# A new order of loads in the opening: both k loads, both q, v, then raw weights on SP, p of the first batch on ScalarE's queue

## The chip, the cores and the metric

The kernel runs on one core of one Trainium2 chip. The metric is the device time of one execution in microseconds (us); several runs give a median. Beside them stands one profiled execution, from which all rows below are read.

## What is computed

Three stages follow each other. Attention of 8 batches of 8 heads, 576 rows of 64, through 32 packed rows `p`; then three products and their maximum, and an output product; then a softplus layer with its output product.

```python
scale = 1.0 / np.sqrt(q.shape[-1])
def sm_attn(qq, kk, vv):
    s = scale * np.matmul(qq, kk.transpose(0, 1, 3, 2))
    s = s - np.max(s, axis=-1, keepdims=True)
    a = np.exp(s)
    a = a / (np.sum(a, axis=-1, keepdims=True) + 1e-09)
    return np.matmul(a, vv)
p_packed = sm_attn(p, k, v)
x = sm_attn(q, p_packed, p_packed)          # then as 4608 x 512
h = np.maximum(np.maximum(x @ w1, x @ w2), x @ w3)
x = h @ w_out
h = x @ w_in
out = (np.maximum(h, 0.0) + np.log1p(np.exp(-np.abs(h)))) @ w_out2
```

## The kernel before

One program works through the batches one after the other. The work of a batch is cut into steps with short names, and a string of names sets the order in which their instructions are written; every engine takes its own instructions in that order. The string of the opening, `order`, holds batch 0 and the preparation of batch 1, beside the narrowing of the weights; the string of the later batches is not touched.

The steps that matter here: `Lk`, `Lq`, `Lv`, `Lp` load k, q, v and p of a batch (`Lk00` and `Lk02` are the two halves of k of batch 0, four heads each; `Lk10`, `Lk12` those of batch 1), `LW` loads a block of a raw weight. `PP` transposes p on TensorE (L269) and ScalarE copies it out of PSUM (L284). `Tk` and `Tq` transpose two heads of k or q (L238, nine matmuls each), and ScalarE or VectorE copies them (L248, L246; the set `on_vector` says which). `S` forms the scores of the packed rows (L311), `SX` their maximum and exponential (L331, L337), `E` transposes those (L358, L365), `V` multiplies with v (L385), `VS` scales (L401), `PT` transposes the packed rows again (L269, L277), `A` forms the scores of q against them (L311), `AX` their exponentials. `PW` multiplies the packed rows with the weights (L486), and `U` are the large products of the second stage (L510). `N` and `NT` narrow a raw weight on ScalarE (L85), GpSimd (L95) and VectorE (L111).

All loads of before are issued by SP, one behind the other. A load waits for one of eight completion semaphores, `DMAHW0` to `DMAHW7`, which are used in turn: a load waits until the load eight places ahead of it has landed. Pools add waits of their own: five buffers for k and q (`rx`), five for raw weights (`stp`), four PSUM tiles (`mm`).

The table `lead` says how many idle transposes of the identity (L166) TensorE does ahead of a step; their results are not read.

Of the kernel before, what the change touches and what calls it, by code (L numbers as in the profile page):

```python
# [19 lines left out]
def packed_attention_maxout_softplus(  # L20
# [22 lines left out]
    nc = tc.nc  # L43
# [113 lines left out]
    ps1, psv, ps2, on_gpsimd, on_vector, lead = {}, {}, {}, set(), set(), {}  # L157
# [51 lines left out]
    def load_p(n):  # L209
        t = tp.tile([P, NG, D], F32, tag="praw", name="praw")  # L210
        for G in range(NG):
            nc.sync.dma_start(
                out=t[:, G],
                in_=bass.AP(p.tensor, p[n, G].offset, [[NG * NP * D, NH], [D, NP], [1, D]]),
            )
        praw[n] = t
# [416 lines left out]
    def opening(name):  # L633
# [20 lines left out]
        if a == "L":  # L654
            return layer2_steps(0, i[1])
        return {
            "Lv": lambda n: once(load_v, n),
            "Lp": lambda n: once(load_p, n),
            "PP": prep_steps,
            "S": lambda n: once(scores1, n),  # L660
# [12 lines left out]

    on_gpsimd.update(
        """
        AX00.sb AX00.mu X00 AX01.sb AX01.mu X01 AX10.sb AX10.mu X10 SO2 SO5 LS02
        LS03 LS04
        """.split()
    )
    on_vector.update("Tk03 Tq00 Tq01 Tq02 Tq03 Tk12".split())  # L680
    lead.update({'Tk00': 12, 'Tk02': 3, 'V0': 14, 'PT0': 3, 'A0': 2, 'Tk10': 14, 'S1': 6, 'U1': 2})
    order = """
            Lk00 Lp0 Lp1 Lk02 LW10 Lq00 Lq02 Tk00 Lv0 LW02 LW00 LW01 PP0 Tk00 Tk01 PP0 Lk10 Tk02
            Tk01 Tk03 Tk02 Lk12 NT10 N10 PP1 Tk03 PP1 S0 N10 LW12 Tq01 SX00 SX01 SX00 LW20 Tq00
            SX01 Tq00 E00 Tq02 VS00 E00 Tq01 E01 Tq02 Tq03 VS01 E01 Tq03 V0 NT02 N02 VS01 VS00
            PT0 N02 PT0 LW11 N00 A0 NT00 PT0 N00 LW21 AX00 NT01 N01 AX00 AX01 AX00 Tk10 AX01
            AX00 N01 AX01 Tk11 Tk10 LW22 AX00 Tk13 AX01 AX00 Tk11 AX00 AX01 Tk12 Tk13 AX01 PW00
            AX01 AX00 N12 Tk12 X00 NT20 S1 AX01 PW00 X00 X01 PW00 N20 U1 X01 SX10 N11 U0 N20
            SX10 NT11 U0 LW30 SX11 N21 NT21 E10 N11 U0 NT12 U1 E10 LW32 N21 NT22 U2 N22 LW31 N12
            U2 SX11 LW50 N22 PW01 LW41 VS11 NT30 N30 U1 E11 PW01 U2 U3 NT32 PW01 N32 U3 E11 U7  # L690
            VS10 N31 N32 NT31 LW40 N31 U3 U6 LS00 LW42 N30 NT50 N50 LW51 LS00 PW02 U6 N50 NT41
            N41 U5 LO3 U7 PW02 N41 LW52 U4 PW02 N40 NT40 N40 U11 LO1 U4 NT42 N42 U5 U8 N42 LS01
            NT51 LO0 N51 LS01 PW03 N51 SO3 ST3 LO2 U8 U9 PW03 Lv1 SO3 SO3 NT52 LO4 PW03 U10 N52
            N52 U9 ST1 U12 LS02 LO5 SO3 Lq11 SO1 LS02 U10 PW04 SO1 U12 U14 ST0 PW04 Lq10 U11 ST2
            SO1 PW04 LS03 U13 SO1 SO2 LS03 SO0 SO2 U15 SO0 SO2 U13 SO2 SO0 U16 U14 U15 SO0 V1
            LS04 U16 ST4 SO4 LS04 U17 VS11 VS10 SO5 SO4 Lq13 ST5 PT1 SO4 U17 LS05 SO5 SO4 SO5
            Lq12 PT1 LS05 SO5 L21 Tq10 Lp2 Tq11 PW10 L21 Lk20 Tq13 L22 PW10 PW10 Lk21 Tq12 D0
            Lk23 A1 L22 D1 L20 AX10 AX10 AX11 AX10 AX11 AX10 AX11 AX10 AX11 AX10 L23 L20 AX11 AX10
            D2 AX11 Lk22 AX10 AX11 X10 X10 AX11 X11 X11 L23
    """  # L700
    E = mybir.EngineType
    under_way = {}
# [128 lines left out]
    def in_batch(n, name):  # L831
# [8 lines left out]
        if a == "Lp":  # L840
            return once(load_p, m + 1) if m + 1 < B else none
# [516 lines left out]
```

## Time and profile before

| | before |
|---|---|
| median of 3 runs | 1206.23 us (1204.69 to 1206.42) |
| profiled execution | 1205.73 us, span 1203.9 us |
| TensorE busy in the span | 1186.9 us, 99% |
| VectorE, ScalarE, GpSimd busy | 837.1, 528.6, 228.2 us |

TensorE is busy almost throughout, and of its 17 us without work most lie ahead of 45 us. The time of the profiled execution is 1.8 us longer than its span, and 0.5 us below the median. Times in the rows count from the start of the span. The granted clock is given as a share of 2.4 GHz: 1.00 is that level, 0.50 is 1.2 GHz.

### The profile page before, as it was taken

To read this page: it belongs to the slowest core of one execution; us is meant where nothing else is said; L and a number is where in the kernel's file an instruction comes from. 1 tells how busy PE (TensorE), PEld (TensorE's weight loads), DVE (VectorE), ACT (ScalarE), POOL (GpSimd) and SP (SyncE) were. 2 spreads that over 40 slices of the span, in tenths; PEclk is the share of its full clock that TensorE was granted. 3 is DMA by queue.
4 is the path that set the end of the run, shared out by engine and by line. 5 is a ranking of instruction groups with operands and counts; after the bars stand their busy time and mean duration, and the time that the engine had idled before them with its cause. 6 is when DMAs were issued, how large, how long until landed. Compare 5 with 4: busy or idle time off the path is not lost.

```text
span 1203.9 us, 21042 instructions
## 1 busy us (share of the span) xinstructions
PE 1186.9 (99%) x8458; PEld 1051.1 (87%) x8458; DVE 837.1 (70%) x1199; ACT 528.6 (44%) x789; POOL 228.2 (19%) x229
## 2 busy tenths in 40 slices
PE   8999999999999999999999999999999999999998
PEld 6788989898989898988888888888888899999998
DVE  3867777677776757777797457974479745874585
ACT  3744453535353624544463234543345333543343
POOL 1732332333233301151000220001200012001100
PEclk8999999999999999999999999999999999999999
DMA  9799879889898721666676955569565697778775
GB/s 274 260 219 221 238 224 238 233 222 248 219 249 218 211 92 34 243 236 258 209 247 187 330 184 184 197 188 336 198 198 173 194 368 250 241 250 325 250 251 148
DMA packets 146818, 272.24 MB, mean 226 GB/s; under 512 B 15136, under 2 KB 88352, under 8 KB 141600
## 3 DMA queue, kind: packets, MB, share of 16 engines
q1 hardware_dynamic: 144512, 269.13, 72.0%
q10 hardware_dynamic: 2208, 1.77, 0.5%
q8 instruction: 66, 1.08, 0.4%
q14 instruction: 32, 0.26, 0.1%
HBM read 218.43 MB, written 52.43 MB: 225 GB/s over the span
## 4 chain that ended last, share of the span: by engine, by line
PE 88%; DVE 5%; DMA 4%; SPq 1%; ACT 1%; issue 1%; POOL 0%; DVEq 0%; ACTq 0%; POOLq 0%
PE ps L510 29%; PE ps L1092 28%; PE ps L1187 25%; PE ps_w L486 3%; DMA woraw<-in_moe_w_out_dram 1%; DMA vt<-in_v_dram 1%; DVE glo L127 1%; PE ps_s L311 1%; DVE x2lo L127 1%; PE ps_v L385 1%; DMA wc<-wic 1%; SPq L187 1%; PE ps_e L358 1%; DVE a L1150 0%; DMA kraw<-in_k_dram 0%
## 5 line engine op out<-in xcount | busy, mean ns | idle before, releaser
L1092 PE MATMUL ps<-x2hi,wc 128*128 128x512 f32 (+1 forms) x1120 | 322.2, 367 | 0.6 <-DMA wc<-wic 0.4
L1187 PE MATMUL ps<-ghi,wc 128*128 128x512 f32 (+1 forms) x1120 | 321.6, 367 | 0.0
L1107 DVE TENSOR_TENSOR h<-h,ps 128x512 f32<-128x512 f32 (+1 forms) x280 | 171.4, 632 | 159.8 <-PE ps L1092 94.1
L1092 PEld LDWEIGHTS ps<-x2hi,wc 128*128 128x128 f32 x1120 | 207.2, 188 | 27.6 <-ACT h L1109 0.7
L1187 PEld LDWEIGHTS ps<-ghi,wc 128*128 128x128 f32 x1120 | 207.1, 188 | 26.0
L1187 PE MATMUL ps<-glo,wc 128*128 128x512 f32 (+1 forms) x560 | 206.6, 369 | 0.7 <-DVE glo L127 0.6
L1092 PE MATMUL ps<-x2lo,wc 128*128 128x512 f32 (+1 forms) x560 | 205.6, 367 | 0.0
L1128 ACT ACTIVATE a<-h 128x512 f32<-128x512 f32 (+1 forms) x160 | 89.0, 585 | 221.6 <-DVE h L1107 194.3
L125 ACT ACTIVATE ghi<-a 128x1024 fp32r<-128x1024 f32 (+1 forms) x120 | 115.8, 974 | 108.5 <-PE ps L1187 99.4
L127 DVE TENSOR_TENSOR glo<-a,ghi 128x1024 fp32r<-128x1024 f32 (+1 forms) x120 | 131.8, 1110 | 33.3 <-ACT ghi L125 33.1
L1150 POOL TENSOR_TENSOR a<-a,a 128x512 f32<-128x512 f32 (+1 forms) x32 | 36.9, 1153 | 537.7 <-ACT a L1128 537.7
L510 PE MATMUL ps<-a2hi,pwhi 128*128 128x288 f32 x576 | 128.4, 304 | 0.4 <-DVE m L540 0.3
L510 PE MATMUL ps<-a2lo,pwhi 128*128 128x288 f32 x576 | 123.2, 295 | 0.9 <-POOL a2lo L127 0.9
L510 PE MATMUL ps<-a2hi,pwlo 128*128 128x288 f32 x576 | 123.3, 295 | 0.0
L1187 PEld LDWEIGHTS ps<-glo,wc 128*128 128x128 f32 x560 | 105.1, 188 | 16.9 <-DVE glo L127 3.6
L1092 PEld LDWEIGHTS ps<-x2lo,wc 128*128 128x128 f32 x560 | 105.1, 188 | 13.2
L510 PEld LDWEIGHTS ps<-a2hi,pwhi 128*128 128x128 f32 x576 | 91.5, 189 | 16.3 <-ACT m L538 6.2
L540 DVE TENSOR_TENSOR m<-ps,m 128x576 f32<-128x576 f32 x96 | 72.4, 754 | 47.2 <-PE ps L510 44.0
L127 POOL TENSOR_TENSOR hlo<-m,hhi 128x576 fp32r<-128x576 f32 x44 | 66.0, 1501 | 199.8 <-ACT hhi L125 181.1
L510 PEld LDWEIGHTS ps<-a2lo,pwhi 128*128 128x128 f32 x576 | 92.4, 188 | 1.4 <-POOL a2lo L127 1.4
L510 PEld LDWEIGHTS ps<-a2hi,pwlo 128*128 128x128 f32 x576 | 92.5, 188 | 0.0
L510 PE MATMUL ps<-hhi,wo_hi 128*128 128x288 f32 x384 | 83.2, 298 | 0.2 <-ACT wo_hi L125 0.2
(121 smaller groups left out, 1485.9 us busy)
## 6 DMA issues: line engine op xcount, KB each, us to landing
wc<-woc SPq DMA_DIRECT2D x40, 1792.0 KB
wc<-wic SPq DMA_DIRECT2D x32, 1792.0 KB
qraw<-in_q_dram SPq DMA_DIRECT2D x112, 140.0 KB
wic<-wc SPq DMA_DIRECT2D x8, 1792.0 KB
kraw<-in_k_dram SPq DMA_DIRECT2D x96, 140.0 KB
wraw<-in_moe_w_dram SPq DMA_DIRECT2D x18, 512.0 KB
xu<-x2d SPq DMA_DIRECT2D x72, 128.0 KB
raw<-in_moe_w_out_dram SPq DMA_DIRECT2D x16, 512.0 KB
```

Of the source, the lines that this page charges most:

```text
L125: nc.scalar.activation(out=hi, in_=src, func=AF.Copy)
L127: engine.tensor_tensor(out=lo, in0=src, in1=hi.bitcast(F32), op=ALU.subtract)
L187: queue.dma_start(out=t[row : row + 32].rearrange("p t b d -> p (t b d)")[:, :size], in_=bass.AP(src.tensor, src[n, NG * g + G].offset + 3 ...
L311: nc.tensor.matmul(ps[G][cols, h, :HS], w[2][rows, G, cols] if 2 in w else w[1][rows, cols], x[rows, g, hh * HS : hh * HS + HS], start=Tru ...
L486: nc.tensor.matmul(ps[cols, G, : units * P].rearrange("p (w x) -> p w x", w=units), ppT[n][1][rows, cols], wsb[rows, 4 * c : 4 * c + units ...
L510: nc.tensor.matmul(o, w, xx, start=first, stop=last)
L540: nc.vector.tensor_tensor(out=m, in0=ps[:, :, :HS], in1=ms[n, f], op=ALU.max)
L1092: nc.tensor.matmul(out, l, r, start=(i == 0), stop=(i == len(terms) - 1))
L1107: add(out=h[:, o], in0=h[:, a], in1=ps, op=ALU.add)
L1128: nc.scalar.activation(out=g[half, k][:, j, :wide], in_=h[:, 2 * k + half], func=AF.Softplus)
L1150: engine.tensor_tensor(out=out, in0=in0, in1=in1, op=op)
L1187: nc.tensor.matmul(ps[b][:, :wide], l, r, start=first and u == 0 and head, stop=u == FP - 1 and tail, skip_group_check=not first,)
```

## The change

The two DMAs of p of batch 0 are issued by ScalarE instead of SP. The string `order` is another, from its first word to the last; the sets `on_gpsimd` and `on_vector` and the table `lead` change with it (56 idle transposes before, 54 now). The steps themselves are the same, and from the first `U` of batch 1 on TensorE's instructions stand in the same order as before.

```diff
     def load_p(n):
         t = tp.tile([P, NG, D], F32, tag="praw", name="praw")
         for G in range(NG):
-            nc.sync.dma_start(
+            (nc.scalar if n == 0 else nc.sync).dma_start(
...
-    on_vector.update("Tk03 Tq00 Tq01 Tq02 Tq03 Tk12".split())
-    lead.update({'Tk00': 12, 'Tk02': 3, 'V0': 14, 'PT0': 3, 'A0': 2, 'Tk10': 14, 'S1': 6, 'U1': 2})
+    on_vector.update("Tk01 Tk03 Tq02 Tq03 Tk12".split())
+    lead.update(
+        {'PP0': 9, 'Tk01': 2, 'Tk02': 6, 'V0': 8, 'PT0': 3, 'A0': 3, 'Tk10': 4, 'PP1': 7, 'PW00': 2, 'E11': 10}
+    )
     order = """
-            Lk00 Lp0 Lp1 Lk02 LW10 Lq00 Lq02 Tk00 Lv0 LW02 LW00 LW01 PP0 Tk00 Tk01 PP0 Lk10 Tk02
...
+            Lp0 Lk00 Lk02 Lq00 Lq02 Lv0 PP0 LW01 PP0 LW02 Tk01 Tk00 LW10 Tk02 Tk00 Tk01 Lk10
...
```

SP's queue from its first load on, before:

```order
L177 DMA kraw_123<-in_k_dram 128x1152
L212 DMA praw_125<-in_p_dram 128x1x64 x2
L212 DMA praw_128<-in_p_dram 128x1x64 x2
L177 DMA kraw_131<-in_k_dram 128x1152
L608 DMA wraw_133<-in_moe_w1_dram 128x4x256
L177 DMA qraw_135<-in_q_dram 128x1152
L177 DMA qraw_137<-in_q_dram 128x1152 [waits DMAHW0_49]
L204 DMA vt_161<-in_v_dram 32x8x384 [waits DMAHW1_49]
L204 DMA vt_161<-in_v_dram 32x8x384 [waits DMAHW2_49]
L204 DMA vt_161<-in_v_dram 32x8x384 [waits DMAHW3_49]
L608 DMA wraw_165<-in_moe_w3_dram 128x4x256 [waits DMAHW4_49]
L608 DMA wraw_167<-in_moe_w1_dram 128x4x256 [waits DMAHW5_49]
```

SP's queue from its first load on, now:

```order
L177 DMA kraw_126<-in_k_dram 128x1152
L177 DMA kraw_128<-in_k_dram 128x1152
L177 DMA qraw_130<-in_q_dram 128x1152
L177 DMA qraw_132<-in_q_dram 128x1152
L204 DMA vt_134<-in_v_dram 32x8x384 x2
L204 DMA vt_134<-in_v_dram 32x8x384 [waits DMAHW0_49]
L608 DMA wraw_152<-in_moe_w2_dram 128x4x256 [waits DMAHW1_49]
L608 DMA wraw_156<-in_moe_w3_dram 128x4x256 [waits DMAHW2_49]
L608 DMA wraw_180<-in_moe_w1_dram 128x4x256 [waits DMAHW3_49]
L177 DMA kraw_201<-in_k_dram 128x1152 [waits DMAHW4_49]
L177 DMA kraw_225<-in_k_dram 128x1152 [waits DMAHW5_49,PE_49]
L608 DMA wraw_255<-in_moe_w1_dram 128x4x256 [waits DMAHW6_49]
```

The two loads of p of batch 0 have left the queue, those of batch 1 have moved to places 13 and 14, and the first raw weight stands behind v instead of ahead of q. Of three raw weights and a load of k behind v, two (`DMAHW1`, `DMAHW3`) wait for the two halves of p of batch 0, which ScalarE issues.

ScalarE's queue from its first instruction on, before:

```order
L70 ACT_TABLE_LOAD
L248 ACTIVATE vT_176<-ps_k_139 128x576 [waits PE_49]
L284 ACTIVATE pT2_188<-ps_t_171 128x256 [waits PE_49]
L248 ACTIVATE vT_176<-ps_k_178 128x576 [waits PE_49]
L248 ACTIVATE vT_176<-ps_k_192 128x576 [waits PE_49]
```

ScalarE's queue from its first instruction on, now:

```order
L70 ACT_TABLE_LOAD
L212 DMA praw_123<-in_p_dram 128x1x64 x2
L284 ACTIVATE pT2_154<-ps_t_138 128x256 [waits PE_49]
L248 ACTIVATE vT_198<-ps_k_170 128x576 [waits PE_49]
L248 ACTIVATE vT_198<-ps_k_182 128x576 [waits PE_49]
```

The two loads of p stand behind the load of the activation tables and wait for nothing.

TensorE's order from its first instruction on, before (`kraw_123` and `kraw_131` are the halves of k, `praw_125` and `praw_128` are p of batch 0 and of batch 1):

```order
L166 MATMUL ps_k_139<-ident_65 128x128 [waits Pool_49]
L166 MATMUL ps_k_139<-ident_65 128x128 x11
L238 MATMUL ps_k_139<-ident_65,kraw_123 128x64 [waits DMAHW0_49]
L238 MATMUL ps_k_139<-ident_65,kraw_123 128x64 x8
L269 MATMUL ps_t_171<-ident_65,praw_125 64x128 [waits DMAHW1_49]
L269 MATMUL ps_t_171<-ident_65,praw_125 64x128
L269 MATMUL ps_t_171<-ident_65,praw_125 64x128 [waits DMAHW2_49]
L269 MATMUL ps_t_171<-ident_65,praw_125 64x128
L238 MATMUL ps_k_178<-ident_65,kraw_123 128x64 x9
L166 MATMUL ps_k_192<-ident_65 128x128 x3
L238 MATMUL ps_k_192<-ident_65,kraw_131 128x64 [waits DMAHW5_49]
```

TensorE's order from its first instruction on, now (`praw_123` is p of batch 0, `kraw_126` and `kraw_128` are the halves of k):

```order
L166 MATMUL ps_t_138<-ident_65 128x128 [waits Pool_49]
L166 MATMUL ps_t_138<-ident_65 128x128 x8
L269 MATMUL ps_t_138<-ident_65,praw_123 64x128 [waits DMAHW1_49]
L269 MATMUL ps_t_138<-ident_65,praw_123 64x128
L269 MATMUL ps_t_138<-ident_65,praw_123 64x128 [waits DMAHW3_49]
L269 MATMUL ps_t_138<-ident_65,praw_123 64x128
L166 MATMUL ps_k_158<-ident_65 128x128 x2
L238 MATMUL ps_k_158<-ident_65,kraw_126 128x64 [waits DMAHW0_49]
L238 MATMUL ps_k_158<-ident_65,kraw_126 128x64 x8
L238 MATMUL ps_k_170<-ident_65,kraw_126 128x64 x9
L166 MATMUL ps_k_182<-ident_65 128x128 x6
L238 MATMUL ps_k_182<-ident_65,kraw_128 128x64 [waits DMAHW2_49]
```

Ahead of the first transposes of k TensorE now waits for both halves of p (`DMAHW1`, `DMAHW3`). The transposes of p of batch 1, which stood ahead of the first scores, stand behind `A0` and the transposes of k of batch 1 now.

## Rows read from the trace of the kernel before

**Rows 1.** Windows of TensorE: window, length and busy (x), granted clock, DMA share, GB/s.

```profile
8.07:14.90 6.83, 5.85 (x70) 0.50 1.06 275
...
22.00:45.00 23.00, 19.71 (x313) 1.00 0.77 254
45.00:98.00 53.00, 51.63 (x517) 1.00 0.90 246
```

**Rows 2.** Timeline of TensorE: start us, us, line, operation, count [idle before <-releaser].

```profile
1.36 2.82 PE L166 MATMUL ps_k<-ident 128*128 128x128 f32 x12 [1.36 <-POOL ident masks.py:199]
4.21 0.94 PE L238 MATMUL ps_k<-ident,kraw 64*128 64x64 f32 x9
...
9.05 1.81 PE L238 MATMUL ps_k<-ident,kraw 64*128 64x64 f32 x18 [2.10 <-DMA kraw<-in_k_dram]
10.80 1.12 PE L269 MATMUL ps_t<-ident,praw 128*64 128x128 f32 x8
11.85 2.17 PE L311 MATMUL ps_s<-vT,pT 64*32 64x288 f32 x32
...
16.61 0.74 PE L238 MATMUL ps_k<-ident,qraw 64*128 64x64 f32 x9 [0.38 <-DMA qraw<-in_q_dram]
...
18.78 1.75 PE L166 MATMUL ps_v<-ident 128*128 128x128 f32 x14
21.93 1.55 PE L385 MATMUL ps_v<-vt,e1T 96*32 96x64 f32 x96 [1.40 <-DMA vt<-in_v_dram]
...
25.46 1.21 PE L311 MATMUL ps_s<-vT,ppT 64*32 64x288 f32 x32 [0.26 <-ACT ppT L284]
```

**Rows 3.** Timeline of the SP queue: start us, us, line, issues.

```profile
0.74 0.41 SPq L177 DMA_DIRECT2D kraw<-in_k_dram  x1
1.21 2.45 SPq L212 DMA_DIRECT2D praw<-in_p_dram  x4
3.70 0.60 SPq L177 DMA_DIRECT2D kraw<-in_k_dram  x1
...
5.83 1.85 SPq L204 DMA_DIRECT2D vt<-in_v_dram  x3
```

**Rows 4.** Timeline of ScalarE, opening.

```profile
0.73 1.28 ACT L70 ACT_TABLE_LOAD   x1 [0.73 <-PEq L1336]
...
18.18 0.81 ACT L365 ACTIVATE e1T<-ps_e 96x768 f32<-96x768 f32 x1 [1.10 <-PE ps_e L358]
```

**Rows 5.** DMA in 2.5:3.5, 4.6:5.0 and 11:14.8: packets (tenths busy ahead in 4.6:5.0).

```profile
DMA packets 87, 0.38 MB, mean 378 GB/s; under 512 B 5, under 2 KB 5, under 8 KB 87
...
DMA  3143143144134135224404413440441399253143
...
DMA packets 119, 0.05 MB, mean 117 GB/s; under 512 B 115, under 2 KB 115, under 8 KB 119
...
DMA packets 390, 0.69 MB, mean 183 GB/s; under 512 B 28, under 2 KB 345, under 8 KB 390
```

**Rows 6.** Issues of ScalarE and of SP after 496 us.

```profile
500.11 0.33 ACTq L588 DMA_DIRECT2D x2d<-xs  x1
...
504.91 0.33 ACTq L588 DMA_DIRECT2D x2d<-xs  x1
...
497.36 1.85 SPq L943 DMA_DIRECT2D wu<-wi  x1
...
500.98 1.16 SPq L943 DMA_DIRECT2D wu<-wi  x1
```

**Rows 7.** DMA by queue in 504.5:506.5, then 509.2:511.5: q1 SP, q10 ScalarE.

```profile
q1 hardware_dynamic: 74, 0.68, 79.8%
q10 hardware_dynamic: 136, 0.28, 36.1%
...
q1 hardware_dynamic: 146, 0.60, 63.5%
q10 hardware_dynamic: 133, 0.27, 30.2%
```

More of the change, by code (lines that the diff above doesn't have):

```diff
@@ L675, in packed_attention_maxout_softplus @@
         """
-        AX00.sb AX00.mu X00 AX01.sb AX01.mu X01 AX10.sb AX10.mu X10 SO2 SO5 LS02
-        LS03 LS04
+        AX00.sb AX00.mu X00 AX01.sb AX01.mu AX10.sb AX10.mu SO2 SO3 LS00 LS01 LS02
+        LS04
         """.split()
     )
-    on_vector.update("Tk03 Tq00 Tq01 Tq02 Tq03 Tk12".split())
-    lead.update({'Tk00': 12, 'Tk02': 3, 'V0': 14, 'PT0': 3, 'A0': 2, 'Tk10': 14, 'S1': 6, 'U1': 2})
+    on_vector.update("Tk01 Tk03 Tq02 Tq03 Tk12".split())
+    lead.update(
+        {'PP0': 9, 'Tk01': 2, 'Tk02': 6, 'V0': 8, 'PT0': 3, 'A0': 3, 'Tk10': 4, 'PP1': 7, 'PW00': 2, 'E11': 10}
+    )
@@ L682, in packed_attention_maxout_softplus @@
     order = """
-            Lk00 Lp0 Lp1 Lk02 LW10 Lq00 Lq02 Tk00 Lv0 LW02 LW00 LW01 PP0 Tk00 Tk01 PP0 Lk10 Tk02
[L684 to L699, printed above, removed]
+            Lp0 Lk00 Lk02 Lq00 Lq02 Lv0 PP0 LW01 PP0 LW02 Tk01 Tk00 LW10 Tk02 Tk00 Tk01 Lk10
@@ new lines, in packed_attention_maxout_softplus @@
+            Tk03 Tk02 Tq00 Tk03 Lk12 S0 Tq03 LW00 SX01 Tq00 Tq01 SX00 SX01 VS01 E01 SX00 Lp1
+            Tq03 E00 E01 VS00 Tq02 E00 Tq02 V0 Tq01 LW20 N01 NT01 VS01 VS00 N01 PT0 NT02 N02
+            LW12 PT0 N02 A0 PT0 LW21 N10 NT10 N10 AX00 LW11 Tk10 AX00 Tk11 Tk10 AX00 AX01 Tk11
+            Tk12 AX01 Tk13 AX00 AX01 Tk12 Tk13 AX00 N00 NT00 AX00 PP1 AX01 N00 AX00 PP1 LW41
+            AX01 PW00 AX00 N20 NT20 S1 X00 AX01 N20 AX01 PW00 LW42 SX11 X00 SX11 AX01 PW00 E11
+            N12 NT21 U0 X01 NT12 VS11 X01 E11 U3 NT11 N11 U0 N12 N21 U3 LW50 N11 U0 NT41 LW40
@@ new lines, in packed_attention_maxout_softplus @@
+            N21 U2 U3 U2 N41 LW22 SX10 PW01 NT42 SX10 N41 PW01 E10 LW31 VS10 U1 NT50 E10 PW01 U1
+            N50 U6 N50 NT40 N42 N40 LW32 N42 U7 LW52 N40 U6 NT22 N22 LW30 U1 U7 PW03 NT31 N31 U2
+            U5 PW03 N22 LW51 N31 LS00 NT32 U4 LO0 PW03 N32 LS00 U4 U14 N52 NT52 N32 U12 LO1 N52
+            NT30 N30 Lv1 U5 N30 U12 U13 LO3 NT51 LO2 LS01 N51 LS01 PW02 U13 U14 U15 PW02 ST0 N51
+            ST1 LS04 LO4 PW02 PW04 U15 LS04 U10 PW04 SO1 PW04 U8 SO0 SO1 LO5 SO0 SO1 Lq10 SO1
+            SO0 U9 U8 SO0 LS02 U11 U9 LS02 U10 Lq12 V1 SO3 ST3 U11 SO3 LS03 ST2 U16 VS11 SO3
@@ L700, in packed_attention_maxout_softplus @@
+            VS10 LS03 SO2 SO3 SO4 PT1 SO2 U17 ST4 PT1 U16 SO2 ST5 SO4 SO5 Lq11 PW10 SO2 SO5 SO4
+            PW10 U17 Lq13 LS05 SO4 LS05 SO5 SO5 L23 Lk21 PW10 Tq10 L20 L23 D0 Tq11 Tq12 Tq13 A1
+            L20 D1 Lk20 L21 AX10 AX10 Lk22 AX11 AX10 AX11 AX10 Lk23 AX11 AX10 AX11 AX10 L22 L21
+            D2 AX11 AX10 AX11 Lp2 AX11 AX11 AX10 X11 X11 X10 X10 L22
     """
```

## Prediction

> **What bounds the kernel now.** The view to begin with is the table of windows: TensorE works 51.63 of the 53 us from 45 to 98 and 19.71 of the 23 us from 22 to 45 [rows 1]. So the time is the work of TensorE plus its holes, and the change can reach only the holes of the opening and what it shifts there. From the first large product of batch 1 on the order on TensorE is the same, so I ask one thing: how much earlier or later does TensorE get there?
>
> The timeline of TensorE gives the holes [rows 2]. It waits for the second half of k until 9.05 (2.10 us), a little for q at 16.61 (0.38 us), and for v until 21.93 (1.40 us); the idle transposes ahead of these, 14 of them from 18.78 in 1.75 us, only fill time in which v had not come either. The granted clock was 0.50, that is 1.2 GHz, from 8.07 to 14.90, after the hole that ends at 9.05, and 1.00 in the windows behind [rows 1]. The SP queue shows why k and v are late: k is issued at 0.74, then four loads of p take 2.45 us of SP, and the second half of k goes out only at 3.70; v at 5.83 [rows 3].
>
> **The change part by part.** 1. *SP gets free earlier.* Without p the second half of k leaves at about 1.2 instead of 3.70. The transfers then lie close: the first half was there at 4.21, when TensorE took it [rows 2], and such a load, 576 KB, lasts 1.56 us at 378 GB/s [rows 5], so the second lands near 5.8, q near 7.3 and 8.9, and v after that. v is 768 packets of 1536 bytes, 48 for each of 16 engines; 390 packets in 3.8 us are 0.156 us each on an engine [rows 5], so 7.5 us: v lands near 16.5, about 5 us before the 21.8 of now. That removes the wait for v, unless something else is late.
>
> 2. *What is late next: p.* The first real work of TensorE in the new order is PP0, which waits for both halves of p. Behind it on TensorE, in order, stand all transposes of k and q, the scores, and V0. The nine idle transposes ahead of it end near 3.5 (12 took 2.82 us from 1.36 on [rows 2]). Call the landing of the second half L; all else hangs on it.
>
> 3. *From L to V0.* The row of PP1, the same eight matmuls at half clock, is 1.12 us [rows 2]. Two idle transposes are 0.47 at half clock, the two k transposes 0.94 and 0.77 (18 of them took 1.81 at half clock, I take 1.71), six idle ones 1.41, the next two k transposes 1.81 at half clock or 2 x 0.74 = 1.48 at full, one of q 0.74, the scores 2.17 at half clock (at 11.85) or 1.21 (the same shape at 25.46). TensorE has stood still before L as it had before 9.05, so I take half clock up to the idle ones and full clock behind: 1.12 + 0.47 + 1.71 + 1.41 + 1.5 + 0.74 + 1.21 = 8.2 us; all at half clock 9.4, all at full clock about 6.7. From the end of the scores to the last copy of the transposed exponentials it was 18.18 + 0.81 - 14.02 = 4.97 us [rows 2, 4], and two transposes of q lie within it as before. Sum: V0 starts at L + 13.2, between L + 11.5 and L + 14.4. The eight idle transposes ahead of V0 lie inside those 4.97 us.
>
> 4. *From V0 on.* PP1 has moved behind V0: at full clock 0.7 us (half of 1.12, and its ends). The idle transposes behind V0 are 29 instead of 27: 0.25 us at 0.125 us (1.75 us for 14 [rows 2]). Some of both lies in holes, since 3.29 us of the window 22 to 45 were empty [rows 1]: between 0 and 0.95, I take 0.6. The narrowing of the first raw weight has its cover: its load is the sixth behind v, near 16.5 + 6 x 1.5 = 25.5, and the product that reads it stands behind A0, which started at 25.46 before and took 1.21, and behind four transposes of k at 0.74 (near 29.6 [rows 2]); without that cover it would cost what it is late.
>
> 5. *The later holes.* 1.37 us lie empty from 45 to 98, and I reckon up to 2 us, with a part of the 3.29 before, as holes that wait for other engines and not for TensorE: a TensorE that comes late loses part of them, one that comes early finds them longer.
>
> **Where L lies.** Nothing in the trace has a load on ScalarE's queue beside loads of SP in the opening, so I bound it. ScalarE's first instruction, the load of the tables, runs from 0.73 to 2.01 [rows 4]. If the issues stand behind it, and take 0.55 to 0.7 each as on SP (2.45 for four [rows 3]), p leaves at 2.05 and 2.65 and begins some 1.1 us after its issue. By then both halves of k and one or both of q have been issued by SP. Two places of the trace show such a meeting. A store of ScalarE issued at 500.11 began only in the window from 504.5, behind the loads that SP had issued from 497.36 on [rows 6, 7]: served in the order of issue, if one reads it so. The store issued at 504.91 ran together with what SP had issued at 500.98: 133 packets against 146 from 509.2 to 511.5 [rows 7], that is one for one.
>
> In the order of issue, p comes behind the second half of k and one or two loads of q: 4.2 + 2 or 3 x 1.56 = 7.3 to 8.9, and its own 64 packets an engine. The two halves are 256 packets of 256 bytes, and only a quarter of the engines are busy with them (tenths 1 to 4, 115 in 0.4 us [rows 5]), so 0.014 us each, 0.9 us. L lies between 7.6 and 9.8; I take 8.7.
>
> **The sum.** V0 at 8.7 + 13.2 = 21.9, as before (21.93); plus 0.6 behind it. Against the profiled execution, 1205.73, this gives 1206.3; that execution lies 0.5 below the median of 1206.23, so **1206.8** for a median. So what v gains, p takes. With L from 7.6 to 9.8 and the bounds of step 3 (-1.7 and +1.2), V0 moves by -2.8 to +2.3: 1204.0 to 1209.1.
>
> **The rivals.**
> *Slower: one packet for one.* If p's 64 packets an engine pass one by one with SP's, each lets one of SP by. From 3.2 on those are some 3 + 8 + 8 + 8 = 27 packets of k and q at 0.195 us (82 large ones in 1 us on 16 engines [rows 5]), 5.3 us, then 37 of v at 0.156, 5.8 us, and 0.9 for p: L = 15.2; 13.9 if p begins 1.3 us earlier. I take 14.5: V0 at 27.7, 5.8 later; plus 0.6, less 1.0 of later holes: +5.4, **1211.6** (L from 13 to 16: +2.9 to +7.9, with the whole 2 us given back at the low end and none at the high one). It decides as soon as L passes 11. For it speaks the even count from 509.2, against it the store that waited its turn at 504.5.
>
> *In runs.* If two packets of p pass for one of SP, 32 pass: 27 x 0.195 + 5 x 0.156 + 0.9 + 3.2 = 10.2, V0 at 23.4, +1.5 + 0.6 - 0.3: **1208.0**. No row shows runs. The Trainium skill, page "DMA: Bandwidth & Descriptors", section "Queues, rings and completion order", has an engine switch between queues only after a packet of typically 9 to 17 descriptors; if the small records here are descriptors, 64 of them would be 4 to 7 turns, and with a k load's eight on the other side (1.56 us) an estimate is L between 9 and 14, a time between the forecast and the slower rival. The even count of rows 7 fits this as well as it fits one for one.
>
> *Early: p is served at once.* If the issues need not wait for the table load they go out at 0.75 and 1.4, with only the first half of k ahead: L = 4.8 to 6.5, V0 at 18.0 to 19.7 (v is there by 16.5), -3.9 to -2.2, plus 0.6, and 0 to 1 comes back in later holes: -3.3 to -0.6, middle -2.0: **1204.2**. With the short bound of step 3 V0 can't pass v at 16.5: -4.8.
>
> *It doesn't do what it says.* v is late for a reason of its own: its packets are slow (183 GB/s against 378 [rows 5]), and if they are as slow again behind q, v lands near 21.8 after all. Then V0 stays and 0.6 is added: **1206.8**.
>
> **How the numbers follow.** Chances: order of issue 0.34, one for one 0.28, early 0.20, in runs 0.12, v no earlier 0.06. A difference of 0.2%, 2.4 us, is about what a measurement of this kernel can tell from none. Slower by more: all of one for one, 0.06 of the runs, 0.04 of the order of issue at its late bound: 0.38. Faster by more: 0.13 of the early case, 0.01 of the order of issue: 0.14. Within: 0.48. The range leaves out the earliest and the latest ends: 1203.0 to 1212.5.
>
> **What would show it.** In the profile of the changed kernel: the second half of k issued near 1.2; the first transposes of p on TensorE end right behind L; V0 13 us behind it, released by the exponentials and no longer by v; the clock at 0.50 after the wait. Step 2 falls if PP0 doesn't wait, step 3 if V0 comes at another distance from PP0, step 4 if the large products of batch 1 begin more than 1 us off what V0 says. The prediction is wrong where L is not between 7 and 11.

## The result, and the profile after

| | before | after |
|---|---|---|
| median | 1205.46 us (4 runs) | 1211.24 us (4 runs, 1210.84 to 1213.03) |
| ratio to before, 95% interval | | 1.0056 [1.0039, 1.0073] |
| span of the profiled execution | 1203.9 us | 1209.2 us |
| V0 starts | 21.93 us | 27.75 us |

The change costs 0.56%, 5.8 us by the medians. It is the rival "one packet for one" (1211.6) that came, not the forecast (1206.8). The time lies inside the range because the range was drawn to take in that rival; for the forecast that is luck.

The timeline of TensorE after the change (start, length, line, operation, count, idle time before and its releaser), to be held against [rows 2]:

```profile
6.00 0.69 PE L269 MATMUL ps_t<-ident,praw 128*64 128x128 f32 x4 [2.45 <-DMA praw<-in_p_dram]
13.52 0.69 PE L269 MATMUL ps_t<-ident,praw 128*64 128x128 f32 x4 [6.83 <-DMA praw<-in_p_dram]
...
14.77 1.81 PE L238 MATMUL ps_k<-ident,kraw 64*128 64x64 f32 x18
...
20.32 2.46 PE L311 MATMUL ps_s<-vT,pT 64*32 64x288 f32 x32
...
27.75 1.55 PE L385 MATMUL ps_v<-vt,e1T 96*32 96x64 f32 x96
```

TensorE takes the first half of p at 6.00 and the second only at 13.52, after 2.45 and 6.83 us of waiting. Everything behind it follows without a hole: V0 starts at 27.75, no longer released by v. The issues were all early. The queue of ScalarE, then of SP, which answer to [rows 3, 4]:

```profile
0.73 1.28 ACT L70 ACT_TABLE_LOAD   x1 [0.73 <-PEq L1338]
0.77 1.74 ACTq L212 DMA_DIRECT2D praw<-in_p_dram  x2
```

```profile
0.74 0.88 SPq L177 DMA_DIRECT2D kraw<-in_k_dram  x2
1.67 0.99 SPq L177 DMA_DIRECT2D qraw<-in_q_dram  x2
2.71 2.02 SPq L204 DMA_DIRECT2D vt<-in_v_dram  x3
```

Both halves of p are issued from 0.77 to 2.51, beside the load of the tables and not behind it; SP has both halves of k out by 1.62, q by 2.66 and v by 4.73. So p is not late because it was asked for late. The DMA by queue (q1 SP, q10 ScalarE: packets, MB, share of 16 engines) in three stretches, 3.7 to 4.4, 4.4 to 6.6 and 6.6 to 12.4 us, shows how it was served:

```profile
q1 hardware_dynamic: 59, 0.24, 93.7%
q10 hardware_dynamic: 109, 0.03, 17.5%
...
q1 hardware_dynamic: 185, 0.77, 95.6%
q10 hardware_dynamic: 23, 0.00, 1.1%
...
q1 hardware_dynamic: 652, 1.42, 102.4%
q10 hardware_dynamic: 130, 0.03, 4.3%
```

109 records of ScalarE's queue in 0.7 us are most of the 128 packets of the first half, in one burst as the first k load ends. The 23 of the next stretch are the other 19, one every 0.19 us on each of their engines, and the four that report the load done. From 6.6 to 12.4 there are 130, the second half with two such reports; the last one starts at 12.50 and has landed at 13.48, and TensorE takes the half at 13.52. A half stands on a quarter of the engines, 32 packets on each, so one every 0.18 us: that is about the 0.195 us of one packet of k, between two of p. In the same stretch SP's queue moved 652, 41 for each of 16 engines. The trace doesn't tell the engines apart, but the pace fits this reading: while SP has loads of its own waiting, about one packet of p passes for each of SP's, although a packet of p alone takes about 0.014 us [rows 5].

### The profile page after: what moved, and what is told of

Read it like the earlier page. It is cut to its first block, busy times and chain, and to the rows that moved or that the text cites. A ratio compares the mean times of both kernels' runs of the same rounds, so it can differ in the third digit from the quotient of the medians.

```text
span 1209.2 us, 21030 instructions
## 1 busy us (share of the span) xinstructions
PE 1187.2 (98%) x8456; PEld 1052.1 (87%) x8456; DVE 837.2 (69%) x1199; ACT 528.9 (44%) x790; POOL 226.3 (19%) x228
## 4 chain that ended last, share of the span: by engine, by line
PE 90%; DVE 5%; DMA 3%; ACT 1%; issue 1%; POOL 0%; SPq 0%; DVEq 0%; ACTq 0%; POOLq 0%
PE ps L510 30%; PE ps L1094 28%; PE ps L1189 25%; PE ps_w L486 3%; PE ps_s L311 1%; DVE glo L127 1%; DMA qraw<-in_q_dram 1%; DMA praw<-in_p_dram 1%; DVE x2lo L127 1%; PE ps_e L358 1%; PE ps_v L385 1%; DMA wc<-wic 1%; PE ps_k L238 1%; DVE a L1152 0%; POOL s L457 0%
```

## Experiments

The theory: *packets*. p on ScalarE's queue passes one by one with SP's packets on the same four engines, TensorE waits for it with all of its opening, and the rest follows. The rivals: *order* (the new order is slow whichever queue p is on), *queue* (a load on ScalarE's queue is slow as such), *bytes* (the amount or the order of issue decides), and *speed* (part of the loss is the half speed of TensorE behind the long wait). All times are ratios to the kernel before, run beside them on the same chip.

| kernel | second half of p taken, us | V0, us | ratio, 95% interval |
|---|---|---|---|
| changed kernel | 13.52 | 27.75 | 1.0056 [1.0039, 1.0073] |
| the same once more | 14.34 | 28.54 | 1.0057 [1.0041, 1.0073] |
| p on SP, ahead of k | 4.53 | 19.04 | 0.9998 [0.9989, 1.0008] |
| p on ScalarE, over 16 engines | 8.55 | 24.85 | 1.0023 [1.0014, 1.0032] |
| PP0 behind the k transposes | 15.46 | 25.70 | 1.0036 [1.0025, 1.0048] |
| before, only p on ScalarE | 7.96 | 21.55 | 1.0008 [0.9995, 1.0020] |
| 84 idle transposes ahead of PP0 | 13.73 | 24.47 | 1.0043 [1.0027, 1.0059] |
| p in twice as many packets | 18.27 | 34.07 | 1.0099 [1.0079, 1.0120] |

### p on SP's queue

```diff
-            (nc.scalar if n == 0 else nc.sync).dma_start(
+            nc.sync.dma_start(
```

> The changed kernel with p of batch 0 on SP's queue again, ahead of the first k load; order, tables and idle transposes unchanged. Theory (packets): p came late because its small packets on ScalarE's queue passed one by one with SP's large ones. Then both halves land near 3.5 to 4.5 here, the first k near 5.3, the scores follow the k and q transposes near 10 and V0 waits for v or the exponentials near 17 to 19: 3 to 5 us earlier than before's 21.9, time 1201 to 1204. Rival (order): the new order is slow whichever queue p is on (late raw weights, PP1 behind A0): then the time stays within 2 us of the changed kernel's 1211.

Timeline of TensorE in this kernel:

```profile
3.47 0.70 PE L269 MATMUL ps_t<-ident,praw 128*64 128x128 f32 x4
4.53 0.69 PE L269 MATMUL ps_t<-ident,praw 128*64 128x128 f32 x4 [0.36 <-DMA praw<-in_p_dram]
...
6.31 1.81 PE L238 MATMUL ps_k<-ident,kraw 64*128 64x64 f32 x18 [0.47 <-DMA kraw<-in_k_dram]
...
11.85 2.21 PE L311 MATMUL ps_s<-vT,pT 64*32 64x288 f32 x32
...
15.80 1.58 PE L358 MATMUL ps_e<-ident,e 128*96 128x128 f32 x12
...
19.04 1.81 PE L385 MATMUL ps_v<-vt,e1T 96*32 96x64 f32 x96
```

Order, tables and idle transposes are those of the changed kernel; only two loads of 32 KB have gone back to SP, ahead of the k loads. p is there at 3.47 and 4.53 and the whole loss is gone: 1.0056 against 0.9998, 0.58%, 7 us. *Order* falls as the cause of the loss. The expected gain over before was missed, though: V0 is 2.9 us earlier than in [rows 2] in the profiled execution, and yet the median is that of before to within 0.1%. A second profile of this kernel says the same of V0:

> The changed kernel with p on SP's queue once more, for a second profile: its first one was the fastest of its 11 executions (1201.36 of a median of 1203.6). If the opening varies, V0 starts later than 19.04, by 1 to 3 us, with TensorE's transposes at the durations of half speed for longer; if not, V0 is within 0.5 us of 19.04 and the spread lies elsewhere.

```profile
19.18 1.21 PE L385 MATMUL ps_v<-vt,e1T 96*32 96x64 f32 x72
```

V0 at 19.18, and 1201.87 us, against 1201.36 in the first profile and 1203.6 in the median of 11 runs. The opening of the kernel before varies too. A second profile of it:

> The kernel before once more, for its profile on the same chip as the runs beside it. If the chip makes no difference, V0 starts at 21.9 and the first large product of batch 1 at 98.1, as in the profile of before; if its opening varies from one execution to the next, they differ by up to 2 us while the large products take the same time.

```profile
8.22 1.60 PE L238 MATMUL ps_k<-ident,kraw 64*128 64x64 f32 x18 [1.03 <-DMA kraw<-in_k_dram]
...
20.23 1.55 PE L385 MATMUL ps_v<-vt,e1T 96*32 96x64 f32 x96 [1.69 <-DMA vt<-in_v_dram]
```

Here the second half of k came 0.8 us and V0 1.7 us earlier than in [rows 2]; this execution took 1204.1 us, the first one 1205.73. So two executions of one kernel differ at V0 by more than half of the 2.9 us between the two kernels. Why the other timed executions of the kernel with p on SP are some 2 us longer than its two profiled ones stays open.

### More packets of the same bytes

```diff
-        for G in range(NG):
-            (nc.scalar if n == 0 else nc.sync).dma_start(
-                out=t[:, G], ...
+        if n == 0:
+            for G in range(NG):
+                for c in range(0, D, D // 2):
+                    nc.scalar.dma_start(out=t[:, G, c : c + D // 2], in_=bass.AP(
+                        p.tensor, p[n, G].offset + c,
+                        [[NG * NP * D, NH], [D, NP], [1, D // 2]]))
```

> The changed kernel with each half of p on ScalarE's queue cut into two loads of 128-byte pieces: 128 packets an engine instead of 64, the same bytes, four issues instead of two (the last ends near 3.2 instead of 2.5). Theory (packets pass one by one): once SP's loads are there each packet of p lets one of SP by, whatever its size. The first 32 go in a burst as before, the other 96 meet q, v and raw weights: p lands at 17 to 22 instead of 13.5, V0 at 31 or later, time 1.008 to 1.013 of before. Rival (bytes or order of issue count): the same bytes, issued 0.7 us later, land by 14.5, time 1.005 to 1.007.

```profile
18.27 0.69 PE L282 MATMUL ps_t<-ident,praw 128*64 128x128 f32 x4 [1.94 <-DMA praw<-in_p_dram]
...
34.07 1.55 PE L398 MATMUL ps_v<-vt,e1T 96*32 96x64 f32 x96
```

```profile
0.77 4.06 ACTq L214 DMA_DIRECT2D praw<-in_p_dram  x4
```

The same 64 KB in pieces half as large land at 18.27 instead of 13.52, and the time goes from 1.0056 to 1.0099. *Bytes* falls: the issues, 0.77 to 4.83, explain at most 2.3 of the 4.75 us (the second row is ScalarE's queue), and the DMA by queue from 6.6 to 15 shows the same pace as above, 191 packets of ScalarE on a quarter of the engines (48 each, one every 0.18 us) beside 911 of SP (57 each on 16):

```profile
q1 hardware_dynamic: 911, 1.81, 97.1%
q10 hardware_dynamic: 191, 0.02, 3.2%
```

### Fewer packets on each engine

```diff
+        if n == 0:
+            for h in range(NH):
+                nc.scalar.dma_start(
+                    out=t[NP * h : NP * h + NP],
+                    in_=bass.AP(p.tensor, p[n, NG * h].offset, [[D, NP], [NP * D, NG], [1, D]]))
```

> The changed kernel with p of batch 0 still on ScalarE's queue, but as four loads by head (32 rows of two pieces of 256 bytes), which I expect to be spread over 16 engines: 16 packets an engine instead of 64. Theory (packets): each passes one by one with SP's, so 16 of SP's go by, 16 x 0.195 = 3.1 us, and the last issue is near 3: p lands by 5.5 to 7, V0 near 19 to 21, time 1203 to 1206. Rival (queue): loads on ScalarE's queue are late as such beside SP's: p lands at 11 or later and the time stays at 1209 to 1212. Rival (order): 1209 to 1212 as well, with p early.

```profile
8.55 1.12 PE L277 MATMUL ps_t<-ident,praw 128*64 128x128 f32 x8 [5.01 <-DMA praw<-in_p_dram]
...
20.27 2.79 PE L366 MATMUL ps_e<-ident,e 128*96 128x128 f32 x12
...
24.85 1.55 PE L393 MATMUL ps_v<-vt,e1T 96*32 96x64 f32 x96
```

Still on ScalarE's queue, at the same time and with as many bytes, p is whole at 8.55 instead of 13.52, and more than half of the loss is gone (1.0023). *Queue* falls. I had expected 5.5 to 7: each of the four loads came about when the SP load that was issued beside it came (landed by 4.5, 6.0, 7.4 and 8.4 us, those of SP by 4.8, 6.3, 8.0 and 10.0). So the packets are not the whole price; what the order of issue adds was not taken apart. V0 is 16.3 us behind p here, where I had 13: the 12 transposes of exponentials at 20.27 still have 2.79 us, where the same 12 had 1.58 with p on SP, so TensorE was at half speed for long (last section).

### The queue alone

```diff
-            nc.sync.dma_start(
+            (nc.scalar if n == 0 else nc.sync).dma_start(
```

This is the kernel before with that one edit.

> The kernel before with p of batch 0 on ScalarE's queue and nothing else changed. On SP there stand then k, the small packets of p of batch 1 (64 on the same four engines) and the second k behind. Theory (packets): p passes mostly against small packets, lands near 5 to 6.5, the second k some 1 us earlier than before, v where it was: time within 2 us of before. Rival (queue): p lands at 10 or later, v waits for p's semaphore and comes later than 21.9: time 1209 or more.

```profile
7.96 0.44 PE L269 MATMUL ps_t<-ident,praw 128*64 128x128 f32 x4 [2.25 <-DMA praw<-in_p_dram]
...
21.55 1.09 PE L385 MATMUL ps_v<-vt,e1T 96*32 96x64 f32 x60 [0.56 <-DMA vt<-in_v_dram]
```

Behind k there stand the small packets of p of batch 1 on SP's queue, not k and q, and the second half comes at 7.96 instead of 13.52, at the same time of issue. V0 stays where v lets it, and the time is that of before within 0.2%. So neither the queue nor the order costs much alone: it is p on the second queue *with large loads of SP right behind it*. p at 7.96 is later than the 5 to 6.5 I expected, and why is not shown.

### PP0 later

```diff
-            Lp0 Lk00 Lk02 Lq00 Lq02 Lv0 PP0 LW01 PP0 LW02 Tk01 Tk00 ...
-            Tk03 Tk02 Tq00 Tk03 Lk12 S0 ...
+            Lp0 Lk00 Lk02 Lq00 Lq02 Lv0 LW01 LW02 Tk01 Tk00 ...
+            Tk03 Tk02 Tq00 Tk03 Lk12 PP0 PP0 S0 ...
-        {'PP0': 9, 'Tk01': 2, ...
+        {'Tk01': 11, ...
```

> The changed kernel with PP0 put behind the transposes of k and the first of q, right ahead of the scores; its idle transposes stand ahead of the first k transpose. p still lands near 13.5. Theory (packets, with all of TensorE queued behind p): k and q are transposed while p comes, the scores start near 14.3 instead of 20.3, V0 near 21 instead of 27.7, time 1204 to 1207. Rival (v or the copies bind in their place): V0 doesn't move by more than 2 us, time 1209 or more.

```profile
15.46 0.69 PE L269 MATMUL ps_t<-ident,praw 128*64 128x128 f32 x4 [4.79 <-DMA praw<-in_p_dram]
16.64 2.17 PE L311 MATMUL ps_s<-vT,pT 64*32 64x288 f32 x32 [0.48 <-ACT pT L284]
...
25.70 1.55 PE L385 MATMUL ps_v<-vt,e1T 96*32 96x64 f32 x96
```

The transposes of k and q are done while p comes, and the time falls from 1.0056 to 1.0036. The scores can't start before p (16.64): by the middle values, what TensorE had queued behind p in vain is about a third of the loss, and the rest is p itself; the two intervals overlap, so this share is rough. V0 came at 25.70 and not at 21, since p was whole at 15.46 in this execution and the scores, 2.17 us, and the transposes behind them ran at half speed.

### TensorE kept at work

```diff
-        {'PP0': 9, 'Tk01': 2, ...
+        {'PP0': 84, 'Tk01': 2, ...
```

> The changed kernel with 84 idle transposes ahead of PP0 instead of 9, so that TensorE works from 1.36 until p's second half lands near 13.5. Theory (half speed behind the wait is a part of the price): p lands as before, but the transposes and scores behind it run at full speed (18 transposes in 1.5 instead of 1.8 us, the scores in 1.2 instead of 2.5, 12 transposes of exponentials in 1.6): V0 near 25 instead of 27.75, time 2 to 3 us below the changed kernel's, so 1.003 to 1.004 of before. Rival (speed is no part of it): V0 within 0.7 us of 27.75 and a time of 1.005 to 1.007 of before.

```profile
14.46 1.14 PE L238 MATMUL ps_k<-ident,kraw 64*128 64x64 f32 x18
...
17.78 1.72 PE L311 MATMUL ps_s<-vT,pT 64*32 64x288 f32 x32
...
24.47 1.55 PE L385 MATMUL ps_v<-vt,e1T 96*32 96x64 f32 x96
```

With p whole at 13.73, as late as in the changed kernel, 18 transposes of k take 1.14 us instead of 1.81 and the scores 1.72 instead of 2.46, and V0 comes at 24.47: 3.3 us sooner. So *speed* is a part of the distance from p to V0. In the time it is 1.0043 against 1.0056, and the intervals overlap; how much of the loss it is in a typical execution is not settled.

The same with p on SP, with 14 idle transposes instead of 9:

> The changed kernel with p of batch 0 first on SP's queue, and 14 idle transposes ahead of PP0 instead of 9, which fill the wait for p's second half (0.36 us in the run with 9). Theory (a small hole costs TensorE its full speed): the transposes and scores run at full speed earlier, V0 near 17.5 instead of 19.04, time 0.999 or below. Rival: the five transposes change nothing or cost their own 0.6 to 1.2 us: time 1.000 to 1.001.

```profile
4.54 0.82 PE L269 MATMUL ps_t<-ident,praw 128*64 128x128 f32 x8
...
5.69 1.14 PE L238 MATMUL ps_k<-ident,kraw 64*128 64x64 f32 x18
...
10.21 1.20 PE L311 MATMUL ps_s<-vT,pT 64*32 64x288 f32 x32
...
17.65 1.78 PE L385 MATMUL ps_v<-vt,e1T 96*32 96x64 f32 x96 [1.11 <-issue]
```

Five idle transposes close the hole of 0.36 us, 18 transposes take 1.14 instead of 1.81 us and the scores 1.20 instead of 2.21, and V0 comes at 17.65, 1.4 us sooner. The ratio is 0.9991 [0.9979, 1.0003]: not told apart from before, nor from the 0.9998 with 9. The last variant has the first k load ahead of p on SP and PP0 behind two k transposes:

> The changed kernel with p of batch 0 on SP's queue behind the first k load, and PP0 behind the first two k transposes, 12 idle transposes ahead of these and 3 ahead of the next: the opening of the kernel before with the new order of the loads. Theory (SP's queue in the new order, without p passing against it, gains what v gains): the second k is there near 6.5, v near 17, V0 near 17 to 18.5 instead of 21.9, time 0.997 to 0.999 of before. Rival (what comes earlier at V0 is lost behind it): V0 earlier by 3 us or more and a time within 0.1% of before.

```profile
19.11 1.55 PE L385 MATMUL ps_v<-vt,e1T 96*32 96x64 f32 x96
```

V0 came at 19.11, later than I expected, ratio 0.9995 [0.9985, 1.0006]. Three variants with p on SP bring V0 3 to 4 us ahead of [rows 2], and none is measurably faster than before. It is not that the gain is lost behind V0: from there to the end of the span the three profiled executions take 1180.6, 1181.9 and 1181.0 us, and the two of the kernel before 1182.0 and 1182.1. But each of the three was the fastest of its 11 or 12 executions (1201.36, 1201.25 and 1201.88 us, where the medians are 1203.6, 1203.92 and 1204.26), so its V0 may not stand for the others. No version here beats the kernel before.

### The changed kernel again

> The changed kernel once more, with more executions and a second profile on one chip. If one profile speaks for the rest, p's halves are taken at 6.0 and 13.5 and V0 starts at 27.75 again, within 1 us, and the ratio to before is 1.004 to 1.007. If the opening varies from one execution to the next as it did in the two profiles of before (V0 at 21.93 and 20.23), V0 differs by 1 to 2 us.

```profile
14.34 0.69 PE L269 MATMUL ps_t<-ident,praw 128*64 128x128 f32 x4 [7.33 <-DMA praw<-in_p_dram]
...
28.54 1.55 PE L385 MATMUL ps_v<-vt,e1T 96*32 96x64 f32 x96
```

The ratio is the same, 1.0057, and p and V0 are 0.8 us later than in the first profile: the first one stands for the rest, to within a microsecond.

## Why the prediction was right and wrong

*That all hangs on L, the landing of p's second half* (step 2): right. With the queue of p as the only difference the loss is there or not (1.0056 and 0.9998).

*Where L lies*: this step failed. I took the order of issue, L at 8.7; it was 13.52 and 14.34, outside the 7 to 11 that I had set as the sign of being wrong. The two meetings of [rows 6, 7] allowed both readings, and I gave more weight to the store that had waited its turn than to the even count, 133 against 146. Both were there in fact: the first half came in a burst when the first k load was done, the second passed one by one with q and v. The slower rival had 13.9 to 15.2 from 64 packets passing one by one from 3.2 us; there were 32 of the second half, and they began at 6.6. Its V0 of 27.7 is so close to 27.75 by luck: L was 1 us earlier than the 14.5 it took, and the way from L to V0 1 us longer. The runs of several packets for one that the Trainium skill would allow (page "DMA: Bandwidth & Descriptors", section "Queues, rings and completion order") don't show in the second half: one record of p every 0.18 us; the burst of the first half, 109 in 0.7 us or some 27 on each engine, could be such a run, but no experiment asked for its cause.

*The load of the tables*: I held it possible that it delays the issue of p. It doesn't: 0.77, within its 1.28 us. What would have made the early case did happen, and p was late all the same.

*Step 1, v earlier*: V0 no longer waited for v in the changed kernel, as forecast. With p early I gave this 0.6 to 3.3 us (V0 at 18.0 to 19.7): with p on SP, V0 came at 19.04 and 19.18 in two profiled executions, but the median shows no gain.

*Step 3, from L to V0*: 14.2 us in both profiles, forecast 13.2 (11.5 to 14.4). The term that was short is the scores, 2.46 instead of the 1.21 of full speed: half speed lasted past the idle transposes.

*Step 4, behind V0*: forecast 0.6 us longer; it was 1.2 us shorter, more than 1 us off, so this term failed too, by the sign that I had set for it. The same product of batch 1 (the second group, with `a2lo`) starts 76.96 us behind V0 before and 75.77 after, by the timelines of before and of after:

```profile
98.89 0.53 PE L510 MATMUL ps<-a2lo,pwhi 128*128 128x288 f32 x2 [0.39 <-POOL a2lo L127]
```

```profile
103.52 0.54 PE L510 MATMUL ps<-a2lo,pwhi 128*128 128x288 f32 x2 [0.27 <-DVE a2lo L127]
```

The waits of TensorE from 28 us to there, after the change (engine, line, waited for, us, times, longest), show where it went:

```profile
PE ps_w L486 <- DVE wsb L111: 1.4, 1, 1.4
PE ps_e L358 <- ACT e L337: 1.3, 2, 0.9
PE ps L510 <- DVE a2lo L127: 0.3, 1, 0.3
PE ps L510 <- ACT a2hi L125: 0.2, 1, 0.2
```

New are most of the 1.4 us ahead of PW00, for a raw weight that VectorE narrows late in the new order (0.3 before), and 1.3 for the exponentials of batch 1; gone are, beside waits for copies of transposes, those of before for v of batch 1 and for the output weights:

```profile
71.25 1.55 PE L385 MATMUL ps_v<-vt,e1T 96*32 96x64 f32 x96 [0.47 <-DMA vt<-in_v_dram]
...
78.09 0.54 PE L510 MATMUL ps<-hhi,wo_hi 128*128 128x288 f32 x2 [0.21 <-ACT wo_hi L125]
...
80.80 0.53 PE L510 MATMUL ps<-hhi,wo_lo 128*128 128x288 f32 x2 [0.60 <-POOL wo_lo L127]
```

These three are 1.28 us. *Step 5* took it that a late TensorE finds such holes filled. The runs show something else: with p on SP, V0 is 8.7 us earlier, and the waits up to the same product are still those of the changed kernel, 1.5 us in the first of the four rows and the same digits in the others, with none of the three holes; it starts 75.95 us behind V0:

```profile
PE ps_w L486 <- DVE wsb L111: 1.5, 1, 1.5
```

```profile
94.99 0.53 PE L510 MATMUL ps<-a2lo,pwhi 128*128 128x288 f32 x2 [0.27 <-DVE a2lo L127]
```

So what is shorter behind V0 comes with the new order, however late TensorE is. In the kernel before, the second profile has V0 1.7 us earlier, and of the three holes only that for v is longer, 0.97 us instead of 0.47. The sum by rows: V0 5.82 later, 1.19 less behind it, 4.63 at the start of batch 1; the spans differ by 5.3, and the 0.7 us between lie in the work behind, whose order is the same.

*The chances*: slower had 0.38, within 0.2% had 0.48. The reading of two meetings far from the opening decided between them, and it deserved no lead.

## What to carry to other kernels

A small load of many short packets on a second queue is not free of the first queue's traffic. Here, while that had large packets waiting, each short one let about one large one by, so the landing went by the number of packets on an engine more than by the bytes. Put such a load ahead of the large ones on the same queue (0.9998 here), or, less good, spread it over all engines (1.0023), and keep the engine that everything else is queued on from waiting for it first. And a kernel's opening varies by a microsecond or two from one execution to the next: one profile with an earlier milestone is no gain until the time shows it.

## What the runs showed that I had not expected

The granted clock reads 1.00 all through the opening of the changed kernel, also where TensorE's rows have the durations of half speed. The window 13.6 to 19 (window, length and busy, granted clock, DMA share, GB/s):

```profile
13.60:19.00 5.40, 5.40 (x43) 1.00 1.12 259
```

18 transposes of k took 1.81 us in it, as in the stretch of before that reads 0.50 [rows 1, 2], and 1.14 us with TensorE at work ahead of them. The column also reads 1.00 where the trace holds no record of the clock. The first record, of full speed, begins at 4.66 us in the kernel before, but at 23.98 in the changed one, behind its slow scores and ahead of V0. It begins at 23.33 with p over 16 engines, at 24.55 with PP0 later, at 13.69 with p on SP, and at 4.91 and 6.18 with 14 and 84 idle transposes ahead of PP0; up to there TensorE's rows have the durations of half speed. So the speed in an opening is read from the length of known instructions and from where the first record begins, not from this column. With p on SP and a hole of 0.36 us in the first transposes of p, the transposes of k at 6.31 and the scores at 11.85 had half speed; with five more idle transposes and no hole, both had full speed from 5.69 on. Which of the two a typical execution gets was not seen, and it may be a part of the variation that stays open.
